# Attention over odd batches with its token chunks on the other half of the partitions

## The chip, the cores and the metric

One core of one Trainium2 chip runs the whole program. The metric is the device time of one execution in microseconds; of several runs the median counts. In the profile PE is TensorE's matmul side, PEld its weight loads, DVE VectorE, ACT ScalarE, POOL GpSimd and SP the engine that issues most DMAs.

## The reference

Three stages in a row. `_attn_ref` is a delta-rule attention over 4 batches, 8 heads, 768 tokens and head size 48; `_moe_ref` a gated feed-forward of width 1536 over the 3072 rows of 384; `_moe2_ref` sends every row to one of 8 experts.

```python
def _attn_ref(q, k, v, beta):
    k_n = k / (np.linalg.norm(k, axis=-1, keepdims=True) + 1e-06)
    state = np.zeros((B, H, D, D))
    for t in range(S):
        kt, vt, bt = (k_n[:, :, t], v[:, :, t], beta[:, :, t, None])
        y[:, :, t] = np.einsum('bhd,bhde->bhe', q[:, :, t], state)
        v_old = np.einsum('bhde,bhd->bhe', state, kt)
        state = state + bt[:, :, :, None] * np.einsum('bhd,bhe->bhde', kt, vt - v_old)

x = y.transpose(0, 2, 1, 3).reshape(B * S, H * D)
xn = x / rms(x) * rms_g                       # moe
x = (silu(xn @ w_gate) * (xn @ w_val)) @ w_out
e = argmax(x @ w_gate2)                       # moe2
out = softmax_e * sigmoid(x @ w_output_gate)_e * (relu(x @ w1[e]) @ w2[e])
```

## The kernel before

**Attention** takes 128 tokens of every head per step (6 steps, `m`), in two chunks of 64 (`ch`). The 32 heads are 16 pairs `q` in two groups `g` of 8; of a group, pairs 0 to 3 are of an even batch and 4 to 7 of an odd one. The two heads of a pair (`h`) lie on the two halves of the 128 partitions.

`early(m)` needs no state. It squares and sums the keys (`squares`), works out the keys' products (`gram` with `what == "k"`, 16 matmuls for each quarter `b` of the heads, called `gk` in the trace), and inverts the chunks' triangular matrices on VectorE (`solve`, L232 to L274: a transposition `nb`, a product, 31 rounds of `tmp` and `x`, four transpositions into `ng`). Four `corner` products (`off`) end it.

`late(m, g)` needs the state. It takes the products of keys and queries (`gq`), and then for each chunk the stages of `chain`: `z` (keys times state, 16 matmuls, then a VectorE subtraction into `v`), `u` (inverse times `v`, 16 matmuls, then two ScalarE copies into `right`), `y` (the output, 16 matmuls with all 128 rows of the array, two copies) and `s` (16 matmuls, two VectorE additions). A float32 matmul shows as two records, so a stage has 32.

Which part of TensorE's array a small matmul uses follows from its partitions: the operands' half gives the rows, the output's half the columns. In `gk` and `z` head 0 has the lower rows and the lower columns, head 1 the upper rows and the upper columns. In `u` it is the lower rows with the upper columns, and the reverse. So a stage goes between two of the four quarters. In `y` every matmul has all the rows, and the columns of half `to`, which is one and the same for the whole stage.

**The feed-forward** has 12 blocks of 256 tokens (`block`), 12 pieces `f` each: `up(f)` of 18 matmuls into `gv` (two PSUM buffers), then ScalarE (`th`, `val`), VectorE (`th`, L641), GpSimd (`th`, L642), ScalarE (`h`, L644), GpSimd (`h`, L645), and `down` of 6 matmuls into `po`. Per step of attention there are two blocks. `route` picks the expert and writes the rows to DRAM; at the end `Moe2` plans units of tokens per expert (`plan_full`, whose list of ids `lt_f` is gathered by GpSimd and transposed by TensorE as `pl_f`), fetches weights (`wraw`) and rows (`xg`), and multiplies.

What is emitted when is set by `Weave`, which counts TensorE's time as written in the yields (0.64 for a stage) and lets the side tasks step when their gap has passed. A scheduler then fixes the order of each engine, and every engine keeps its own order. The PSUM tag `at` has 4 banks, shared by all of attention, `xt`, `off` and `rk`; a `z`, `u` or `gk` takes one, a `y` two.

## Time and profile before

| | |
|---|---|
| runs | 1111.62, 1114.97, 1115.9 us (median 1114.97) |
| span of the profiled execution | 1112.2 us |
| PE busy | 1009.8 us, 91% |
| DVE busy | 692.9 us, 62% |
| ACT busy | 468.8 us, 42% |
| POOL busy | 457.0 us, 41% |

The page gives the span of the profiled execution, and not its time apart from that; the three runs lie from 0.6 us below to 3.7 us above this span, their median 2.8 us above it. The slices of the page show three parts: to about 130 us weights and the first inverse, with PE half busy; from there to about 835 us attention and feed-forward together, with PE at 98% and more from 300 us on; then the experts. Whoever reads it should not stay with the share of the whole span: in a stretch of the middle part VectorE is as full as TensorE, and the windows show which.

### The profile page before, as it was taken

The numbers are of one execution on the slowest core, as the hardware profiler recorded it, in microseconds if no ns is written. First come the engines' busy times: TensorE is split into PE (matmuls) and PEld (weight loads), VectorE is DVE, ScalarE is ACT, GpSimd is POOL, SyncE is SP. The second block draws the span as 40 slices with busy tenths as digits, with TensorE's granted clock in tenths as the row PEclk, the third lists the DMA queues.
The fourth block names the chain that finished last, engine by engine and source line by source line (L and its number), as shares of the span: only waits on it lengthen the run. The fifth ranks groups of instructions, "written<-read, shape, count | busy, mean of one in ns | idle before, by whom it ended". The sixth has DMA issues, their size and how long they took to land.

```text
span 1112.2 us, 27509 instructions
## 1 busy us (share of the span) xinstructions
PE 1009.8 (91%) x11189; PEld 953.3 (86%) x11189; DVE 692.9 (62%) x1954; ACT 468.8 (42%) x1193; POOL 457.0 (41%) x523
## 2 busy tenths in 40 slices
PE   5726898899999999999999999999999999999993
PEld 4725797788898989998999889999998889999993
DVE  5995889669833994389536973234418646557550
ACT  6626552353345334533354334333436434445440
POOL 9517443432544335433534243325653553212210
PEclk9999699899999999999999999999999899999997
DMA  9812750122302211220312130001404574355320
GB/s 290 218 58 75 207 114 1 34 70 44 73 16 45 58 45 45 58 59 16 72 45 45 31 72 16 2 2 64 165 1 146 174 236 153 130 192 190 115 99 15
DMA packets 53289, 97.04 MB, mean 87 GB/s; under 512 B 5792, under 2 KB 38198, under 8 KB 50338
## 3 DMA queue, kind: packets, MB, share of 16 engines
q1 hardware_dynamic: 43122, 48.76, 16.6%
q0 software_dynamic: 7680, 45.08, 11.7%
q8 instruction: 90, 1.47, 0.6%
q10 hardware_dynamic: 2352, 1.37, 0.4%
q14 instruction: 45, 0.37, 0.1%
HBM read 83.78 MB, written 12.09 MB: 86 GB/s over the span
## 4 chain that ended last, share of the span: by engine, by line
PE 49%; DVE 21%; issue 11%; POOL 7%; DMA 6%; ACT 4%; SPq 1%; POOLq 0%; ACTq 0%; DVEq 0%
PE gv L632 17%; PE po L655 8%; PE cpo L1010 8%; PE ph L989 8%; DVE tmp L253 5%; DVE x L257 5%; PE y L332 2%; POOL raw L520 1%; POOL th L642 1%; DVE th L641 1%; DMA sq<-in_kv_dram 1%; DVE left L223 1%; PE off L293 1%; DVE right L343 1%; POOL h L645 1%
## 5 line engine op out<-in xcount | busy, mean ns | idle before, releaser
L642 POOL TENSOR_TENSOR th<-th,val 128x256 f32<-128x256 f32 x144 | 111.1, 773 | 268.9 <-DVE th L641 227.9
L655 PE MATMUL po<-wout,h 128*128 128x400 f32 x864 | 192.4, 353 | 4.0 <-ACT h L644 2.8
L641 DVE SCALAR_TENSOR_TENSOR th<-th,gv 128x256 f32<-128x256 f32 x144 | 60.1, 417 | 176.3 <-ACT val L640 170.5
L644 ACT ACTIVATE h<-th 128x256 fp32r<-128x256 f32 x144 | 60.0, 417 | 241.3 <-POOL th L642 241.2
L632 PE MATMUL gv<-xh,wgv 128*128 128x256 f32 x864 | 150.0, 295 | 7.0 <-DVE th L641 6.8
L655 PEld LDWEIGHTS po<-wout,h 128*128 128x128 f32 x864 | 148.0, 189 | 8.9 <-ACT h L644 3.9
L632 PE MATMUL gv<-xh,wl 128*128 128x256 f32 x864 | 146.2, 287 | 3.3 <-DVE th L641 3.2
L645 POOL TENSOR_TENSOR h<-th,h 128x256 fp32r<-128x256 f32 x144 | 108.3, 753 | 73.6 <-ACT h L644 73.3
L632 PEld LDWEIGHTS gv<-xh,wgv 128*128 128x128 f32 x864 | 125.3, 197 | 10.4 <-DVE th L641 7.6
L632 PEld LDWEIGHTS gv<-xh,wl 128*128 128x128 f32 x864 | 122.9, 190 | 7.7 <-DVE th L641 5.6
L1010 PE MATMUL cpo<-w2h,ch 128*128 128x384 f32 (+1 forms) x464 | 124.2, 340 | 1.9 <-ACT w2h L950 1.9
L253 DVE TENSOR_TENSOR tmp<-nb,x 128x110 f32<-128x110 f32 (+35 forms) x366 | 106.4, 330 | 4.2
L989 PE MATMUL ph<-xT,w1h 128*128 128x256 f32 (+4 forms) x528 | 95.1, 315 | 0.1
L257 DVE TENSOR_TENSOR x<-x,tmp 128x110 f32<-128x110 f32 (+35 forms) x366 | 94.4, 295 | 0.3
L638 ACT ACTIVATE th<-gv 128x256 f32<-128x256 f32 x144 | 54.5, 378 | 79.5 <-PE gv L632 77.2
L1010 PEld LDWEIGHTS cpo<-w2h,ch 128*128 128x128 f32 (+1 forms) x464 | 81.8, 184 | 4.3 <-ACT w2h L950 2.5
L989 PEld LDWEIGHTS ph<-xT,w1h 128*128 128x128 f32 x528 | 82.9, 192 | 1.7 <-DVE ch L994 0.4
L632 PE MATMUL gv<-xl,wgv 128*128 128x256 f32 x432 | 79.6, 291 | 1.0 <-DVE xl L613 1.0
L1010 PE MATMUL cpo<-w2l,ch 128*128 128x384 f32 (+1 forms) x232 | 78.2, 338 | 0.0
L632 PE MATMUL gv<-xl,wl 128*128 128x256 f32 x432 | 77.0, 285 | 0.0
L632 PEld LDWEIGHTS gv<-xl,wgv 128*128 128x128 f32 x432 | 64.9, 197 | 1.9 <-DVE xl L613 1.4
L994 DVE SCALAR_TENSOR_TENSOR ch<-ph,ch 128x512 fp32r<-128x512 f32 (+4 forms) x64 | 39.0, 611 | 40.9 <-ACT ch L993 40.9
(241 smaller groups left out, 1841.8 us busy)
## 6 DMA issues: line engine op xcount, KB each, us to landing
kT<-in_kqT_dram SPq DMA_DIRECT2D x24, 192.0 KB, 3.8
raw<-in_wo_dram SPq DMA_DIRECT2D x12, 384.0 KB, 7.4
left<-in_kqT_dram SPq DMA_DIRECT2D x24, 192.0 KB, 4.2
v<-in_kv_dram SPq DMA_DIRECT2D x12, 384.0 KB, 3.4
k<-in_kv_dram SPq DMA_DIRECT2D x24, 192.0 KB, 4.9
raw<-in_wg_dram SPq DMA_DIRECT2D x12, 384.0 KB, 3.4
raw<-in_wv_dram SPq DMA_DIRECT2D x12, 384.0 KB, 4.3
rows<-y SPq DMA_DIRECT2D x10, 385.0 KB, 3.0
```

Source lines behind the costliest of these rows:

```text
L253: nc.vector.tensor_tensor(out=t, in0=nb[:, k + 1:, k:k + 1].to_broadcast([P, n, b - a]), in1=x[:, k:k + 1, a:b].to_broadcast([P, n, b - a] ...
L257: nc.vector.tensor_tensor(out=x[:, k + 1:, a:b], in0=x[:, k + 1:, a:b], in1=t, op=ALU.add)
L632: nc.tensor.matmul(out=ps[:, gv], lhsT=self.weight(wi, cc, gv, slice(f * P, f * P + P)), rhs=xx[:, cc], start=i == 0, stop=i == 8)
L638: nc.scalar.activation(out=th, in_=ps[:, 0], func=AF.Tanh, scale=0.5)
L641: nc.vector.scalar_tensor_tensor(out=th, in0=th, scalar=1.0, in1=ps[:, 0], op0=ALU.add, op1=ALU.mult)
L642: nc.gpsimd.tensor_tensor(out=th, in0=th, in1=val, op=ALU.mult)
L644: nc.scalar.activation(out=h2[:, 0], in_=th, func=AF.Copy)
L645: nc.gpsimd.tensor_tensor(out=h2[:, 1], in0=th, in1=h2[:, 0].bitcast(F32), op=ALU.subtract)
L655: nc.tensor.matmul(out=po[t], lhsT=h[:, ts], rhs=self.wo[wi][:, f], start=f == 0 and i == 0, stop=f == 11 and i == 2)
L989: nc.tensor.matmul(out=ph[:, fl], lhsT=w1[wi][:, cc, f * P:(f + 1) * P], rhs=xt[:, xi, cc], start=i == 0, stop=i == 8)
L994: nc.vector.scalar_tensor_tensor(out=hl, in0=ph, scalar=0.0, in1=hh.bitcast(F32), op0=ALU.max, op1=ALU.subtract)
L1010: nc.tensor.matmul(out=po[t][0:rows[t]], lhsT=hs[f // 2][:, hi, f % 2, t * P:t * P + rows[t]], rhs=w2[wi][:, f], start=f == 0 and i == 0, ...
```

## The change

For the heads of odd batches (pairs 4 to 7 of a group, `f` = 1 in the new code) the two heads' chunks lie on swapped halves of the partitions: in `v`, `k`, `ng`, the gram matrices, `beta`, the tokens' ids and the output `x`. The host arrays are reordered to fit. In `z`, `u` and the new `keygram` even and odd pairs then alternate over all four quarters of the array, each parity into a PSUM bank of its own; in `y` they alternate between the two halves of the columns. `keygram` does two quarters of the heads at once (32 matmuls, two banks). Nothing is added to or taken from the matmuls themselves. `gq`, `s` and `off` keep their pattern.

Around it: `z` is subtracted in two VectorE operations of half the size, `u` copied in four ScalarE operations of half the size, the keys `k` are loaded by three DMAs in place of two, the grams of step 1 by four in place of two, and a block's rows are written by three DMAs in place of one (step 0: four in place of two). The yield after the keys' products is 0.8 for both quarters (twice 0.64 before).

```diff
+    def keygram(self, m, g):
+        bank = [self.ps.tile([P, 8, 64], F32, tag="at", name=f"gk{m}{g}{f}") for f in range(2)]
+        for pl in range(4):
+            for ch in range(2):
+                for f in range(2):
+                    for h in range(2):
+                        kk = k[64 * h:64 * h + D, 4 * f + pl, 64 * ch:64 * ch + 64]
+                        o = 64 * (h ^ f)
+                        nc.tensor.matmul(out=bank[f][o:o + 64, 2 * pl + ch], lhsT=kk, rhs=kk, start=True, stop=True)
...
+        turns = [(i, f, 4 * f + i, h) for i in range(4) for f in range(2) for h in range(2)]
+        if stage in "zu":
+            bank = [self.ps.tile([P, 4, D], F32, tag="at", name=f"{stage}{m}{ch}{g}{f}") for f in range(2)]
         if stage == "z":
-            for q in range(GPR):
+            for i, f, q, h in turns:
+                nc.tensor.matmul(out=bank[f][own[h ^ f], i], lhsT=kT[sub[h], q, 64 * ch:64 * ch + 64],
+                                 rhs=R[sub[h], q, h], start=True, stop=True)
+            for f in range(2):
+                v = vn[:, 4 * f:4 * f + 4]
+                nc.vector.tensor_tensor(out=v, in0=v, in1=bank[f], op=ALU.subtract)
+        elif stage == "u":
+            for i, f, q, h in turns:
+                nc.tensor.matmul(out=bank[f][own[1 - h], i], lhsT=self.ng[own[h ^ f], 2 * (g * GPR + q) + ch],
+                                 rhs=vn[own[h ^ f], q], start=True, stop=True)
+            for f in range(2):
                 for h in range(2):
-            nc.vector.tensor_tensor(out=vn, in0=vn, in1=ps, op=ALU.subtract)
-            for h in range(2):
-                nc.scalar.activation(out=R[own[1 - h], :, h], in_=ps[own[1 - h]], func=AF.Copy)
+                    nc.scalar.activation(out=R[own[1 - h], 4 * f:4 * f + 4, h], in_=bank[f][own[1 - h]], func=AF.Copy)
...
-            o = own[to]
-            for q in range(GPR):
+            for i in range(4):
                 for h in range(2):
-                    nc.tensor.matmul(out=bank[q // 4][o, q % 4, h], lhsT=self.left[g][:, q, h, 64 * ch:64 * ch + 64],
-                                     rhs=R[:, q, h], start=True, stop=True)
+                    for f in range(2):
+                        q = 4 * f + i
+                        nc.tensor.matmul(out=bank[f][own[to ^ f], i, h],
+                                         lhsT=self.left[g][:, q, h, 64 * ch:64 * ch + 64],
+                                         rhs=R[:, q, h], start=True, stop=True)
...
-            nc.sync.dma_start(out=rows[m * P:(m + 1) * P, 2 * g:2 * g + 2], in_=y)
+            nc.sync.dma_start(out=rows[m * P:(m + 1) * P, 2 * g], in_=y[:, 0])
+            for h in range(2):
+                nc.sync.dma_start(out=rows[m * P + 64 * h:m * P + 64 * h + 64, 2 * g + 1],
+                                  in_=y[64 - 64 * h:128 - 64 * h, 1])
```

Three places in the engines' orders. On PE, the last step's inverse products of group 0 (`u`), before, among the feed-forward's `gv`:

```order
L632 MATMUL gv_7907<-xh_7559,wgv_82 128x256 x3
L319 MATMUL u_7917<-v_4_6576,ng 64x48 x16
L208 MATMUL gk_7936<-ek_5_7791 64x64 x16
L632 MATMUL gv_7907<-xh_7559,wgv_81 128x256 x3
L632 MATMUL gv_7907<-xl_7560,wgv_81 128x256 x3
```

and of the changed kernel, where `u_8046` and `u_8047` are the banks of the even and the odd batch:

```order
L659 MATMUL gv_8036<-xh_7626,wgv_82 128x256 x3
L340 MATMUL u_8046<-v_4_6675,ng 64x48 x2
L340 MATMUL u_8047<-v_4_6675,ng 64x48 x2
L340 MATMUL u_8046<-v_4_6675,ng 64x48 x2
L340 MATMUL u_8047<-v_4_6675,ng 64x48 x2
```

The 16 matmuls of `u` are now pairs that alternate between two banks, and the keys' products no longer follow them directly: both `keygram`s stand apart, the one ahead of this `u`, the other after the next `y`.

On DVE, the start of the last inverse, before: `nb` is its first transposition, `th` the feed-forward's product, one per piece `f`, and the last `th` here is that of piece 6 of block 7.

```order
L641 SCALAR_TENSOR_TENSOR th_8053<-th_8053,gv_8034 128x256
L343 TENSOR_TENSOR right_78<-right_78,s_8062 48x8x48 x2
L243 MEMSET x_8256 128x1024
L238 STREAM_TRANSPOSE nb_8170<-xr_7868 128x1024
L244 MEMSET x_8256 128x32
L240 TENSOR_TENSOR nb_8170<-nb_8170,naT_8144 128x1024
L314 TENSOR_TENSOR v_4_6576<-v_4_6576,z_8119 128x8x48
L253 TENSOR_TENSOR tmp_0_8277<-nb_8170,x_8256 128x31
L257 TENSOR_TENSOR x_8256<-x_8256,tmp_0_8277 128x31
L253 TENSOR_TENSOR tmp_1_8280<-nb_8170,x_8256 128x30 x2
L257 TENSOR_TENSOR x_8256<-x_8256,tmp_1_8280 128x30 x2
L641 SCALAR_TENSOR_TENSOR th_8155<-th_8155,gv_8109 128x256
```

and of the changed kernel, where `th_8185` is that of piece 5 and `th_8238` that of piece 6:

```order
L668 SCALAR_TENSOR_TENSOR th_8084<-th_8084,gv_8036 128x256
L263 MEMSET x_8389 128x1024
L264 MEMSET x_8389 128x32
L258 STREAM_TRANSPOSE nb_8292<-xr_7980 128x1024
L369 TENSOR_TENSOR right_78<-right_78,s_8194 48x8x48 x2
L668 SCALAR_TENSOR_TENSOR th_8185<-th_8185,gv_8122 128x256
L260 TENSOR_TENSOR nb_8292<-nb_8292,naT_8280 128x1024
L273 TENSOR_TENSOR tmp_0_8398<-nb_8292,x_8389 128x31
L668 SCALAR_TENSOR_TENSOR th_8238<-th_8238,gv_8219 128x256
```

The transposition has moved one piece earlier, while the rounds behind it stand about where they did.

On POOL, the fetches of the first plan after the last `y`, before (`lt_f` is the list of ids, `wraw` the experts' weights):

```order
L645 TENSOR_TENSOR h_10560<-th_10554,h_10560 128x256
L940 DMA wraw_10327<-in_w_dram,wi_f 128x3072
L940 DMA wraw_10328<-in_w_dram,wi_f 128x3072
L782 DMA lt_f<-list,li_f 6x128
L642 TENSOR_TENSOR th_10588<-th_10588,val_10590 128x256
```

and of the changed kernel:

```order
L672 TENSOR_TENSOR h_10713<-th_10707,h_10713 128x256
L813 DMA lt_f<-list,li_f 6x128
L971 DMA wraw_10480<-in_w_dram,wi_f 128x3072
L971 DMA wraw_10481<-in_w_dram,wi_f 128x3072
L669 TENSOR_TENSOR th_10741<-th_10741,val_10743 128x256
```

The list has moved ahead of the two weights. On PE, `pl_f`, which transposes it, stands 80 feed-forward matmuls after the last `y`, where 153 stood between them before.

## Rows read from the trace of the kernel before

**Rows 1.** The page: the span.

```profile
span 1112.2 us, 27509 instructions
```

**Rows 2.** Busy time by stretch: start:end, length, then each engine's us (instructions).

```profile
240.00:302.00 62.00, 60.21 (x766) 56.08 (x765) 59.77 (x189) 20.87 (x58) 22.82 (x27) 1.00 0.28 65
...
601.00:648.00 47.00, 45.32 (x524) 41.61 (x522) 45.90 (x169) 15.33 (x45) 15.38 (x20) 1.00 0.16 44
sum 206.00, PE 199.33 PEld 184.79 DVE 200.31 ACT 67.02 POOL 70.53; mean PE 49.83 PEld 46.20 DVE 50.08 ACT 16.75 POOL 17.63
...
648.00:770.00 122.00, 122.00 (x1583) 115.02 (x1583) 44.44 (x137) 47.36 (x127) 47.54 (x70) 1.00 0.09 21
```

**Rows 3.** Groups of PE instructions, 220 to 770 us: records, busy us, mean ns.

```profile
L332 PE MATMUL y<-right,left 128*64 128x48 f32 x640 | 44.0, 224 | 0.6 <-ACT right L322 0.2
L312 PE MATMUL z<-right,kT 48*64 48x48 f32 x626 | 24.4, 220 | 3.2 <-DVE right L343 2.9 <-DVE left L223 0.3
L319 PE MATMUL u<-v,ng 64*64 64x48 f32 x640 | 22.9, 220 | 1.1 <-DVE v L314 1.1
L208 PE MATMUL gk<-ek 48*64 48x64 f32 x512 | 19.1, 221 | 2.7 <-DMA ek<-in_kqT_dram 2.7
```

**Rows 4.** Timeline of PE, 584 to 594 us: start, length, rows*columns used, records.

```profile
584.95 0.96 PE L319 MATMUL u<-v,ng 64*64 64x48 f32 x26
585.70 0.27 PE L208 MATMUL gk<-ek 48*64 48x64 f32 x2
585.74 0.28 PE L319 MATMUL u<-v,ng 64*64 64x48 f32 x3
585.80 0.22 PE L208 MATMUL gk<-ek 48*64 48x64 f32 x1
585.81 0.22 PE L319 MATMUL u<-v,ng 64*64 64x48 f32 x1
585.81 0.22 PE L208 MATMUL gk<-ek 48*64 48x64 f32 x1
585.86 0.22 PE L319 MATMUL u<-v,ng 64*64 64x48 f32 x1
585.86 0.22 PE L208 MATMUL gk<-ek 48*64 48x64 f32 x1
585.87 0.22 PE L319 MATMUL u<-v,ng 64*64 64x48 f32 x1
585.87 0.98 PE L208 MATMUL gk<-ek 48*64 48x64 f32 x27
...
589.13 2.07 PE L332 MATMUL y<-right,left 128*64 128x48 f32 x32
591.12 1.15 PE L208 MATMUL gk<-ek 48*64 48x64 f32 x32
```

**Rows 5.** Timeline of PE, 409 to 428 us: a `u` and what follows.

```profile
411.17 1.14 PE L319 MATMUL u<-v,ng 64*64 64x48 f32 x32 [0.39 <-DVE v L314]
412.24 0.86 PE L632 MATMUL gv<-xh,wgv 128*128 128x256 f32 x5
```

**Rows 6.** The four stretches of Rows 2, instructions that use tile y alone.

```profile
sum 206.00, PE 20.18 PEld 18.05 DVE 3.34 ACT 10.32; mean PE 5.04 PEld 4.51 DVE 0.83 ACT 2.58
```

**Rows 7.** Timeline of PE and of POOL, 764 to 790 us: the last `y`, the plan.

```profile
764.65 1.83 PE L332 MATMUL y<-right,left 128*64 128x48 f32 x28
...
787.18 0.22 PE L791 MATMUL pl_f<-ident,lf_f 6*128 6x6 f32 x1
...
775.73 0.96 POOL L782 DMA_INDIRECT lt_f<-list,li_f  x1 [0.30 <-issue]
```

**Rows 8.** DMA issues: count and us to landing.

```profile
lt_f<-list,li_f POOLq DMA_INDIRECT x1, 8.1
lt_m<-list,li_m POOLq DMA_INDIRECT x1, 3.0
```

**Rows 9.** Timeline of PE, 95 to 119 us: a `y` of the first step.

```profile
96.85 4.91 PE L332 MATMUL y<-right,left 128*64 128x48 f32 x46
```

More of the change, by code (lines that the diff above doesn't have):

```diff
@@ L77, in load @@
             for h in range(2 if n > 0 else 0):
-                nc.sync.dma_start(
-                    out=self.left[g][64 - 64 * h:128 - 64 * h, 0:4 * n, h],
-                    in_=a["kq", m][64 * h:64 * h + 64, 16 * g:16 * g + 8 * n].rearrange("p (q c) t -> p q (c t)", c=2))
+                for f in range(n):
+                    o = 64 * (h ^ f)
+                    nc.sync.dma_start(
+                        out=self.left[g][64 - 64 * h:128 - 64 * h, 4 * f:4 * f + 4, h],
+                        in_=a["kq", m][o:o + 64, 16 * g + 8 * f:16 * g + 8 * f + 8].rearrange(
+                            "p (q c) t -> p q (c t)", c=2))
         else:
@@ L199, in gram @@
         g = b // 2
-        ps = self.ps.tile([P, 8, 64], F32, tag="at", name=f"g{what}{m}{b}")
-        k, left = T["early", g] if what == "k" else T["kT"][g], self.left[g]
+        ps = self.ps.tile([P, 8, 64], F32, tag="at", name=f"gq{m}{b}")
+        k, left = T["kT"][g], self.left[g]
         for pl in range(4):
@@ L364, in early @@
                 self.nc.sync.dma_start(out=T["raw"][1][r, ns], in_=self.a["kk", m][r, q % 2, ns])
-        for b in range(4):
-            if b >= n:
-                self.gram(m, b, "k")
-            if not ready:
-                self.roots(m, b)
-            yield (0.64 if b >= n else 0.0), eg
+        for g in range(2):
+            if 2 * g >= n:
+                self.keygram(m, g)
+            for b in (2 * g, 2 * g + 1):
+                if not ready:
+                    self.roots(m, b)
+            yield (0.8 if 2 * g >= n else 0.0), 2 * eg
         if not ready:
@@ L725, in route @@
         if m:
-            nc.sync.dma_start(out=rows[m * P:(m + 1) * P, 2 * g:2 * g + 2], in_=y)
+            nc.sync.dma_start(out=rows[m * P:(m + 1) * P, 2 * g], in_=y[:, 0])
+            for h in range(2):
+                nc.sync.dma_start(out=rows[m * P + 64 * h:m * P + 64 * h + 64, 2 * g + 1],
+                                  in_=y[64 - 64 * h:128 - 64 * h, 1])
         else:
             for h in range(2):
-                nc.sync.dma_start(out=rows[64 * g:64 * g + 64, 2 * h:2 * h + 2], in_=y[64 * h:64 * h + 64])
+                for t in range(2):
+                    nc.sync.dma_start(out=rows[64 * g:64 * g + 64, 2 * (h ^ t) + t], in_=y[64 * h:64 * h + 64, t])
         run = small("run", [P, 2, 8])
@@ L1070, in constants @@
     iota("cnt0", [P, 8], [[NT, 8]], 0, 0)
[L1071 removed]
+    c["tok"] = pool.tile([P, NM, 2, 2], I32, name="tok")
     c["tok0"] = pool.tile([P, 2, 2], I32, name="tok0")
     for h in range(2):
[L1075 removed]
+        p = slice(64 * h, 64 * h + 64)
+        for t in range(2):
+            nc.gpsimd.iota(c["tok"][p, :, :, t], pattern=[[P, NM], [2 * S, 2]], base=64 * (h ^ t) + S * t,
+                           channel_multiplier=1, allow_small_or_imprecise_dtypes=True)
+        nc.gpsimd.iota(c["tok0"][p], pattern=[[64, 2], [-S if h else 3 * S, 2]], base=2 * S * h, channel_multiplier=1,
                        allow_small_or_imprecise_dtypes=True)
```

62 lines of the change are left out of this document (29 added, 33 removed).

## The prediction, as put on record

> **What bounds the kernel now.** I read the windows first, since the share of the whole span mixes stages. From 220 to 770 us, where attention and feed-forward run together, TensorE is full: in the last 122 us before the attention ends it is busy for all of them, VectorE for 44 [rows 2]. There a microsecond off TensorE is a microsecond off the kernel. But in four stretches, 206 us in all, one per inverse of steps 2 to 5, VectorE is busy for 200.3 us and TensorE for 199.3 [rows 2]. The reader is to see that both are at 97% there: what is taken from TensorE is then waited for at VectorE, since `gv` has two buffers and each piece `f` needs VectorE's `th`. So the first question is how much shorter the small matmuls get, the second where they stand.
>
> **What a stage costs, and why.** A `u` of 32 records starts at 411.17, and the next matmul at 412.24: 1.07 us [rows 5]. Within a stage 26 records take from 584.95 to 585.70, 28.8 ns each [rows 4], so 32 of them are 0.92 us, and 0.15 us is what a stage loses at its end. `y` takes 1.99 us for 32 records (589.13 to 591.12), and with 0.13 to 0.15 us at its end 58 ns each: twice the time of `u` for as many columns streamed [rows 4]. `u` goes between two quarters of the array, `y` stays in one half of the columns. That is the pattern of a cost per place in the array of 58 ns per record, of which two places hide each other's.
>
> **Would four places hide four?** The trace holds the experiment by accident. Where `gk` follows `u` directly, the last `u` and the first `gk` run mixed. `u` uses the two quarters that `gk` doesn't. From 585.70 to 585.87 start 2+3+1+1+1+1+1+1 = 11 records, 15.5 ns each [rows 4], against 28.8 while `u` is alone just before and (585.87 on, 27 records of `gk`) again just after. Four quarters work at once, and two that share their rows and differ in columns don't hold each other up. The rate is 15.5 / 28.8 = 0.54 of that of two, near a half.
>
> The Trainium skill's page "TensorE: Matmul & The Clock Gate" (Part 3, "The mechanism") has a rule against this change: weight loads overlap running matmuls only where the row groups differ. By it `y`, whose matmuls have all the rows, gains nothing, and `z`, `u` and `gk`, which change rows already, little; the kernel would stay at about 1115. The mixed records above speak against that rule for the quarters; for `y`, with all 128 rows, no row here shows it.
>
> **The change part by part.**
>
> *`z` and `u`.* 32 records at 15.5 ns are 0.50 us, with 0.15 at the end 0.65, against 1.07: 0.42 saved; at an exact half 0.46. I take 0.43. From 220 to 770 us there are 626 / 32 and 640 / 32, so 20 of each [rows 3]: 40 x 0.43 = 17.2 us.
>
> *`y`.* The trace has no `y` that alternates columns. The bounds are 0 (the all-rows matmul doesn't overlap) and 32 x 29.2 + 150 ns = 1.08, so 0.91 saved of 1.99. It is nearest to the mixed rows, where tiles that share rows and differ in columns run side by side, so I take 0.54 of the rate with some loss, 0.88. 20 of them [rows 3]: 17.6 us.
>
> *`gk`.* 512 / 32 = 16 stages [rows 3] become 8 of double size. Two are 2 x 1.07; the double one is 64 x 15.5 + 150 ns = 1.14: 1.0 saved; where a `gk` mixed with its neighbour before, some 0.15 of that was had already. I take 0.9: 7.2 us.
>
> Together 42.0 us of TensorE's time between 220 and 770.
>
> *What VectorE takes back.* In the four stretches lie 20.18 of the 44.0 busy us of `y` [rows 3, 6], 46%; by the order `z` and `u` lie there in much the same share, while all `gk` lie outside (the inverse comes after them). 0.45 x (17.2 + 17.6) = 15.7 us of the saving falls where VectorE has 200.3 of 206 us to do. At most 5.7 us of idle can go there. I take 2, because its rounds have waits of their own, and because the first transposition of each inverse now stands one piece earlier, where VectorE has room. So 42.0 - 15.7 + 2 = 28.3 us. The ends: 42.0 - 15.7 = 26.3 if nothing is recovered, 42.0 if the inverse's operations spread over the pieces so that nothing binds.
>
> *The first step.* Its `u`, `y` and `z` stand before 150 us. One `y` run takes 4.9 us there for 46 records [rows 9], so 2 to 4 us could go; but VectorE and the weights decide when the first block begins. Bounds 0 and 4, I take 1.5.
>
> *The plan.* `pl_f` ran at 787.18, 20.7 us after the last `y` ended (764.65 + 1.83) [rows 7], and TensorE did 153 feed-forward matmuls in between, 0.135 us each. Now 80 stand between: 10.8 us. TensorE's queue stops there until the list is in, and the feed-forward behind it waits too. But the list's fetch, issued at 775.73 and 8.1 us on its way behind two weight fetches, is now ahead of them; the one like it later took 3.0 us [rows 7, 8]. Issued some 2.7 us earlier and landing 5 us sooner, and without the split of the weights that VectorE did ahead of its copy, it comes about 11 us after the last `y`. Cost 0 to 10 us, I take 1.
>
> *The small pieces.* Two half subtractions for one and four half copies for two add an operation's fixed part each; `u` to `y` is still over 20 matmuls of 0.135 us apart, and the same holds from `z` to `u`, so they are hidden outside the stretches. Inside them one more VectorE operation for each of some 9 `z` is below 1 us. The DMAs stand in SP's queue: three for `k` instead of two, three for a block's rows instead of one; ahead of them SP mostly waits for data, and only the last block's rows are on the path, for two more issues. I take 0.5 for all.
>
> Sum: 28.3 + 1.5 - 1 - 0.5 = 28.3 us. From the span of 1112.2 [rows 1] this gives 1083.9, and with the 2.8 us by which the median of the runs lies above it, **1087 us**.
>
> **The rivals.**
>
> *`y` gains nothing* (12 in 100). All rows are taken by each matmul, so the column halves might follow each other. Outside the stretches that takes away 0.55 x 17.6 = 9.7 us: 1096. For it: no row shows such a pair. Against: the quarters that share rows overlap.
>
> *VectorE doesn't bind* (14 in 100). Its rounds are filler whose place the order sets; if they spread over more pieces, all 42 us go, and up to 4 at the start: 1115 - 46 = 1069. For it: in the last 122 us VectorE is at 36% [rows 2], and the inverse begins earlier. Against: in the new order the rounds stand between the same pieces as before.
>
> *The columns don't overlap at all* (10 in 100). What the mixed records show might be an effect of two tiles of different stages. Then only the small costs are left: 1113 to 1118. Against: the rate changes with the first mixed record and returns with the last [rows 4].
>
> *The banks run out* (5 in 100), on the other side. `z`, `u` and `gk` now hold two of the four `at` banks, `y` two as before, so a stage can only start when the one before the last is evacuated. In the stretches VectorE is behind, and holds the banks of `gq` and `z`. 48 stages are affected; from a mean wait of 28.3 / 48 = 0.6 us on, the gain is gone, and at 0.8 us each (38 us) the time is 1125. For it: VectorE is 97% busy where it must free them. Against: `y` takes two banks right after `u` today, with 0.6 us of idle over all `y` [rows 3], and the stages stay over 20 matmuls apart.
>
> The page "TensorEngine Tiling (Array Packing)" of the Trainium skill ("PSUM Bottleneck") says the same in general: tiling speeds up TensorE and not the evacuation, which may become the bound. Here the trace shows VectorE full in 206 of 550 us, by other work than evacuation.
>
> **How the numbers follow.** My forecast has 59 in 100, with its own range of 1076 to 1095 (half of the recoverable cases on either side, the plan's wait above). The range for 8 in 10 reaches from 1067, just below the case in which VectorE doesn't bind, to 1104, beyond that of `y` without gain; what is left out is mostly the 15 in 100 of no overlap and of the banks. A measurement here tells 0.5%, 5.6 us, from no change. Faster by more than that: 59 + 12 + 14 = 85 in 100; within it: 10; slower: 5.
>
> **What would show it.** In the profile of the changed kernel `z` and `u` should take 0.6 to 0.7 us from their first record to the next stage's (1.07 before), `y` 1.05 to 1.2 (1.99), a double `gk` 1.05 to 1.2. If `y` stays at 2.0 it is the first rival; if all stay, the third. The four stretches should still last about as long as before, with VectorE at 97% and more, and TensorE at 90% or less in them, idle before `gv` and `z` with VectorE as the releaser. The 122 us that end at 770 should shrink by about 4 x 0.43 x 2 + 5 x 0.88 = 8 us. `pl_f` should follow the last `y` by 11 to 12 us, with less than 2 us of idle before it. I am wrong if TensorE waits for banks (idle before `z`, `u` or `gk` released by an evacuation), if the stretches shrink by more than 6 us in all, or if the inverse now ends so late that `off` waits.

## The result, and the profile after

The changed kernel takes 1123.53 us (1120.97 to 1125.13, 6 runs) against 1115.16 us (1111.31 to 1118.29, 6 runs) for the kernel before: ratio 1.0076, 95% interval 1.0054 to 1.0097. It is slower by 8.4 us where 28 us of gain were forecast, and the forecast range of 1067 to 1104 doesn't hold it.

The page of the changed kernel, span and engines, for [rows 1]:

```profile
span 1121.0 us, 27686 instructions
...
PE 990.6 (88%) x11189; PEld 926.9 (83%) x11189; DVE 702.3 (63%) x1976; ACT 473.7 (42%) x1241; POOL 458.4 (41%) x526
```

The window from 220 to 770 us, first the kernel before, then the changed one (columns as in [rows 2], the third from the end is the mean granted clock):

```profile
220.00:770.00 550.00, 539.00 (x7241) 502.69 (x7237) 335.78 (x1047) 219.33 (x591) 222.56 (x274) 1.00 0.17 42
```
```profile
220.00:770.00 550.00, 513.53 (x7079) 472.49 (x7070) 339.31 (x1040) 218.99 (x617) 222.03 (x262) 0.96 0.18 41
```

TensorE is busy for 25.5 us less in the same 550 us, at a granted clock of 0.96 in place of 1.00. The two windows don't hold quite the same work, so I also took the account between the same two feed-forward pieces, from VectorE's `th` of piece 6 of block 1 to that of piece 0 of block 10. That part took 529.6 us and takes 536.1. TensorE's busy time in it went from 518.6 to 500.5, idle from 11.0 to 35.7; and of the 500.5, up to 19.9 us are lost to clocks below 1.00 (an estimate: one minus the granted clock, summed over TensorE's busy time; 1.7 before). So 18.1 + 18.2 = 36 us of work at full clock were taken away, less than the 42 forecast, and 24.7 us of idle and 18.2 of lower clock took their place. Some 3 of the 36 us are no saving: a `u` and two of the keys' stages that lay in this part now run ahead of it.

The small matmuls themselves. Groups of PE's instructions between 220 and 777 us, changed kernel, for [rows 3]:

```profile
L355 PE MATMUL y<-right,left 128*64 128x48 f32 x640 | 32.5, 235 | 11.7 <-ACT right L344 11.3
L333 PE MATMUL z<-right,kT 48*64 48x48 f32 x608 | 17.0, 223 | 5.0 <-DVE left L243 3.4 <-DVE right L369 1.6
L340 PE MATMUL u<-v,ng 64*64 64x48 f32 x640 | 15.5, 224 | 2.4 <-DVE v L337 2.4
L215 PE MATMUL gk<-ek 48*64 48x64 f32 x451 | 10.5, 247 | 2.0 <-DMA ek<-in_kqT_dram 2.0
```

And single stages on PE's timeline, changed kernel, for [rows 4, 5]:

```profile
354.91 1.15 PE L355 MATMUL y<-right,left 128*64 128x48 f32 x32
355.99 1.16 PE L215 MATMUL gk<-ek 48*64 48x64 f32 x64
357.08 0.39 PE L659 MATMUL gv<-xl,wl 128*128 128x256 f32 x1
...
583.81 0.68 PE L333 MATMUL z<-right,kT 48*64 48x48 f32 x32
584.42 1.35 PE L682 MATMUL po<-wout,h 128*128 128x400 f32 x6
...
588.06 0.68 PE L340 MATMUL u<-v,ng 64*64 64x48 f32 x32
588.67 0.62 PE L659 MATMUL gv<-xh,wgv 128*128 128x256 f32 x3
```

`z` and `u` go from 1.07 to 0.61 us from their first record to the next matmul, `y` from 1.99 to 1.08, and a double `gk` takes 1.09 where two took 2.14. That is what was forecast, where a stage finds its operands and the full clock. The last column of the groups holds the other half: 11.7 us of idle before `y`, where the kernel before had 0.6. PE's waits from 220 to 772 us, changed kernel (what waits, for which engine's product; us in all, times, longest):

```profile
PE y L355 <- ACT right L344: 11.3, 7, 7.5
PE gv L659 <- DVE th L668: 5.3, 4, 2.1
PE po L682 <- ACT h L671: 3.7, 5, 1.4
PE xt L632 <- DVE x L621: 3.4, 4, 1.5
PE z L333 <- DVE left L243: 3.4, 4, 1.4
PE po L682 <- POOL h L672: 2.7, 3, 2.3
PE u L340 <- DVE v L337: 2.4, 5, 0.7
PE gk L215 <- DMA ek<-in_kqT_dram: 2.0, 2, 1.1
PE z L333 <- DVE right L369: 1.6, 2, 1.4
```

These nine sum to 35.8 us. The same list of the kernel before sums to 10.2 us, its longest entry being

```profile
PE z L312 <- DVE right L343: 2.9, 3, 1.1
```

No single wait took the gain; they are spread over ScalarE, VectorE and GpSimd.

Where in the program? I compare the starts of the same feed-forward `th` in both traces. From piece 3 of block 0 to the middle of block 1 the changed kernel is ahead (by 2.7 us at the start of block 1). The four stretches with an inverse, measured between the same pieces, took 206.8 us before and take 219.1: 12.3 us more, in order of time 0.6, 2.4, 4.9 and 4.4. Between them it gains only 5.7 us in all, where 26 were forecast. At the last piece of the feed-forward it is 7.4 us behind, at the end of the span 8.8. The two windows that answer to the last rows of [rows 2], a stretch and the time after it:

```profile
604.00:653.00 49.00, 43.26 (x508) 39.49 (x508) 46.96 (x167) 15.22 (x46) 16.26 (x20) 0.93 0.16 42
653.00:777.00 124.00, 120.44 (x1601) 112.14 (x1601) 47.95 (x149) 49.32 (x138) 49.41 (x71) 0.97 0.09 21
```

VectorE is busy for 47 of 49 us of the stretch, as before, while TensorE is at 43 and its clock at 0.93. Pieces 6 of block 7 to 4 of block 8, which hold this stretch, took 49.8 us and take 54.2.

### The profile page after: what moved, and what is told of

The parts are those of the page before. It is cut to its first block, busy times and chain, and to the rows that moved or that the text cites. A ratio compares the mean times of both kernels' runs of the same rounds, so it can differ in the third digit from the quotient of the medians.

```text
span 1121.0 us, 27686 instructions
## 1 busy us (share of the span) xinstructions
PE 990.6 (88%) x11189; PEld 926.9 (83%) x11189; DVE 702.3 (63%) x1976; ACT 473.7 (42%) x1241; POOL 458.4 (41%) x526
## 4 chain that ended last, share of the span: by engine, by line
PE 43%; DVE 25%; issue 13%; POOL 7%; ACT 6%; DMA 5%; POOLq 0%; SPq 0%; ACTq 0%; DVEq 0%
PE gv L659 13%; PE cpo L1041 8%; PE ph L1020 7%; PE po L682 7%; DVE tmp L273 6%; DVE x L277 6%; POOL th L669 2%; DVE th L668 2%; PE y L355 2%; DVE right L369 1%; POOL raw L547 1%; POOL h L672 1%; ACT xr L221 1%; PE off L310 1%; PE gq L236 1%
## 5 line engine op out<-in xcount | busy, mean ns | idle before, releaser
L669 POOL TENSOR_TENSOR th<-th,val 128x256 f32<-128x256 f32 x144 | 114.4, 795 | 264.8 <-DVE th L668 198.5
L682 PE MATMUL po<-wout,h 128*128 128x400 f32 x864 | 198.8, 361 | 10.6 <-ACT h L671 7.4
L682 PEld LDWEIGHTS po<-wout,h 128*128 128x128 f32 x864 | 151.3, 194 | 18.6 <-ACT h L671 9.4
L659 PE MATMUL gv<-xh,wl 128*128 128x256 f32 x864 | 148.8, 292 | 9.5 <-DVE th L668 9.4
L659 PEld LDWEIGHTS gv<-xh,wl 128*128 128x128 f32 x864 | 125.8, 195 | 14.6 <-DVE th L668 12.7
L277 DVE TENSOR_TENSOR x<-x,tmp 128x110 f32<-128x110 f32 (+35 forms) x366 | 101.9, 315 | 0.2
L665 ACT ACTIVATE th<-gv 128x256 f32<-128x256 f32 x144 | 54.2, 376 | 74.8 <-PE gv L659 71.9
```

The costliest lines, as they stand in the source:

```text
L277: nc.vector.tensor_tensor(out=x[:, k + 1:, a:b], in0=x[:, k + 1:, a:b], in1=t, op=ALU.add)
L659: nc.tensor.matmul(out=ps[:, gv], lhsT=self.weight(wi, cc, gv, slice(f * P, f * P + P)), rhs=xx[:, cc], start=i == 0, stop=i == 8)
L665: nc.scalar.activation(out=th, in_=ps[:, 0], func=AF.Tanh, scale=0.5)
L669: nc.gpsimd.tensor_tensor(out=th, in0=th, in1=val, op=ALU.mult)
L682: nc.tensor.matmul(out=po[t], lhsT=h[:, ts], rhs=self.wo[wi][:, f], start=f == 0 and i == 0, stop=f == 11 and i == 2)
```

## The experiments

All ratios are against the kernel before, run beside it on the same chip; us are worked out from them with 1115. Chips differ by up to 14 us (medians of the kernel before from 1115 to 1129), so spans from different chips aren't set side by side. The starts of feed-forward pieces are: what follows the last piece takes 278 to 283 us in the traces of the faster chips and 288 to 292 in those of the slower, so most of the difference lies there.

### The turns, and what came with them

**paired** keeps the new layout, the two banks and the double `keygram`, but runs the even batch's matmuls first and then the odd one's:

```diff
-        turns = [(i, f, 4 * f + i, h) for i in range(4) for f in range(2) for h in range(2)]
+        turns = [(i, f, 4 * f + i, h) for f in range(2) for i in range(4) for h in range(2)]
```

(and `f` outermost in `keygram` and `y`).

> The changed kernel with the turns taken back in all four kinds of stages: the layout, the half-size copies and subtractions, the double gk and the DMAs stay, but the matmuls of f = 0 come first and those of f = 1 after them, so only two parts of the array (in y one half of the columns) are used in turn. Theory A (the turns do save TensorE's time, and the idle time that the rest of the change brings eats it): z and u go back to about 1.07 us, y to 2.0, TensorE is busy for some 40 us more, and the kernel is slower than the changed one: 1130 to 1145. Theory B (outside TensorE's queue other engines set the pace everywhere, so TensorE's time is worth nothing): 1119 to 1127, as the changed one. Theory C (the turns themselves do the harm, since a TensorE that waits loses its clock): faster than the changed one, 1112 to 1118.

Measured: 1.0232 [1.0199, 1.0266]. The stages don't go all the way back: undisturbed, `z` and `u` take 0.88 us and a double `gk` 1.84, and a `y` 1.80 (PE, `paired`):

```profile
631.36 1.87 PE L355 MATMUL y<-right,left 128*64 128x48 f32 x32
633.16 1.36 PE L682 MATMUL po<-wout,h 128*128 128x400 f32 x6
```

So between 220 and 770 us the turns alone shorten TensorE's stages by some 31 us (an estimate: 40 x 0.27 + 20 x 0.72 + 8 x 0.75), and the new places alone by the rest. In the kernel's time the turns are a gain, of 1.0232 − 1.0076 = 1.56%, 17.4 us. But everything else in the change costs 2.3%, 26 us, where the prediction had 1.5 (the plan and the small pieces). Some 13 us of what the turns give is had in the first step: at piece 4 of block 0, `paired` is 11.4 us behind the kernel before and the changed kernel 1.5 ahead. There it is the order that differs, and not only the length of the stages: in `paired` the second `u`, both `y` and `s` stand in a row on TensorE, from 137 to 149 us, where the kernel before and the changed one have feed-forward matmuls among them. From there to the last piece the turns are worth 5.6 us more.

Two experiments take one of the other parts alone, without turns, into the kernel before. **before_2bank** gives `z` and `u` two banks and the halved operations behind them:

```diff
-                    nc.tensor.matmul(out=ps[own[h], q], lhsT=kT[sub[h], q, 64 * ch:64 * ch + 64],
+                    nc.tensor.matmul(out=bank[q // 4][own[h], q % 4], lhsT=kT[sub[h], q, 64 * ch:64 * ch + 64],
```

> The kernel before, in its own layout and with no turns, but z and u write the first four heads' pairs to one bank and the last four to another, with two half subtractions and four half copies, as the changed kernel has to. If the second bank of z is what it waits for (z of the later heads then needs the bank of the second gq, which VectorE frees with the mask that stands behind the inverse's rounds): idle time before z of some 10 us, and 1.006 to 1.012 of the time before. If the half operations and the banks are hidden: 0.998 to 1.003.

Measured: 1.0122 [1.0091, 1.0153], 13.6 us. Of that 8.6 us are there by piece 4 of block 0, where the second `u`, both `y` and `s` now run ahead of the feed-forward, as in `paired`. The waits that I expected before `z` are there, at about half of the size, released by the operation that empties `gq`'s bank (PE's waits, 220 to 772 us, `before_2bank`):

```profile
PE z L314 <- DVE left L223: 5.8, 4, 2.0
```

But they cost nothing where they stand: from piece 6 of block 1 to piece 0 of block 10 this kernel takes 528.7 us, the kernel before 529.6. Another 4.5 us come between that piece and the last. So most of the price arises in step 1, with an order that came with the second bank, and none of it from these waits.

**before_gk2** lets the plan take two of the keys' stages in one step, as the changed kernel does:

```diff
-        for b in range(4):
-            if b >= n:
-                self.gram(m, b, "k")
-            if not ready:
-                self.roots(m, b)
-            yield (0.64 if b >= n else 0.0), eg
+        for g in range(2):
+            for b in (2 * g, 2 * g + 1):
+                if b >= n:
+                    self.gram(m, b, "k")
...
+            yield (0.8 if 2 * g >= n else 0.0), 2 * eg
```

> The kernel before with one edit: two stages of gk are issued in one step of the plan, as the double gk is, each with its bank, copies and places as before, and no turns. If the row of copies and norm steps that comes of it is what the double gk costs: idle time of 5 to 12 us before y with ScalarE as the releaser, 1.005 to 1.012. If it is the double gk's two banks and turns that matter, or nothing: 0.998 to 1.003.

Measured: 1.0098 [1.0063, 1.0134], 10.9 us. Together 24.5 us, about the 26 of `paired`. My expectation of where was wrong, though: `y` doesn't wait here. PE's largest wait in this kernel is for something else, and 6.9 of the 10.9 us lie in the four stretches, which take 213.7 us in place of 206.8:

```profile
PE po L657 <- ACT h L646: 6.5, 6, 2.4
```

### The lump of copies on ScalarE

The longest single wait of the changed kernel is the 7.5 us of a `y` at 230.61. The timelines of POOL, ACT and PE around it, changed kernel, in order of time:

```profile
223.23 3.23 POOL L127 TENSOR_TENSOR nrm<-ss,half 128x8 f32<-128x8 f32 x2 [1.03 <-DVE ss L106]
226.43 0.72 POOL L669 TENSOR_TENSOR th<-th,val 128x256 f32<-128x256 f32 x1
```
```profile
227.18 0.42 ACT L671 ACTIVATE h<-th 128x256 fp32r<-128x256 f32 x1 [4.34 <-POOL th L669]
227.50 0.64 ACT L218 ACTIVATE xr<-gk 128x256 f32<-128x256 f32 x2
...
230.23 1.37 ACT L344 ACTIVATE right<-u 64x192 f32<-64x192 f32 x4
```
```profile
230.61 0.45 PE L355 MATMUL y<-right,left 128*64 128x48 f32 x2 [7.50 <-ACT right L344]
```

The reader is to see a queue, not a slow engine. Two steps of the norms stand on GpSimd ahead of the feed-forward's `th`; ScalarE's `h` waits 4.34 us for it; behind `h` stand the eight copies of a double `gk`, 2.7 us; only then comes the copy of `u` for which `y` waits. Two variants take the lump apart.

**ksplit** makes four single `gk` of the two double ones, each with its own step and yield as before; `z`, `u` and `y` keep their turns:

```diff
-        for g in range(2):
-            if 2 * g >= n:
-                self.keygram(m, g)
-            for b in (2 * g, 2 * g + 1):
+        for b in range(4):
+            if b >= n:
+                self.keygram(m, b // 2, b % 2)
...
-            yield (0.8 if 2 * g >= n else 0.0), 2 * eg
+            yield (0.64 if b >= n else 0.0), eg
```

> The changed kernel with the double gk taken apart again: four stages of gk a step, each with one bank, its four copies and its own step in the plan, as before; z, u and y keep their turns. Theory A1 (the double gk puts eight copies in a row into ScalarE's queue, ahead of the copies of u for which y waits, and two norm steps in a row into GpSimd's): the idle time before y with ScalarE as the releaser falls from 11.3 us to under 3, and the kernel comes to 1104 to 1112, faster than both, although gk costs TensorE 7 us more. Theory A2 (the loss is in the four stretches where VectorE is full, and in the clock there): the idle time before y falls too, but the time stays at 1116 to 1124.

**kevict** keeps the 32 matmuls together and takes only the copies and the norms by halves:

```diff
+        for b in range(4):
+            if b >= n:
+                if b % 2 == 0:
+                    bank = self.keygram(m, b // 2)
+                self.keyraw(m, b // 2, b % 2, bank[b % 2])
```

> The changed kernel with the double gk kept, so that its matmuls go to four places in turn, but its copies and norm steps issued by halves, the second half a step of the plan later, as before. If ScalarE's eight copies and GpSimd's two norm steps in a row are what the double gk costs: like ksplit or better by up to 6 us, 0.993 to 1.001 of the time before, idle time before y under 3 us. If it is the place of the double gk in TensorE's order or the two banks that it holds: 1.004 to 1.010, as the changed kernel.

Measured: `ksplit` 0.9998 [0.9979, 1.0017], `kevict` 0.998 [0.9956, 1.0003]. In `ksplit` the time fell between its two ranges, and `kevict` kept the wait that I expected to go. So a plan step with two stages in it costs 0.8 to 1.0% whether the matmuls are shorter or not. But the lump at 230 us is not where it costs. In `ksplit` all waits of `y` are 1.7 us; in `kevict` that one wait stays (7.7 us), and the time is as good. By the pieces' starts the three kernels part late: at piece 6 of block 7 the changed kernel is 2.0 us behind the kernel before, `ksplit` 2.8 behind and `kevict` 0.4 ahead; at piece 0 of block 9 the changed kernel is 10.5 behind, `ksplit` 1.0 behind and `kevict` 0.6 ahead. The last two stretches take 54.5 and 54.2 us in the changed kernel, 50.2 and 50.0 in `ksplit`, 50.9 and 51.4 in `kevict`. The longest wait was thus not the dearest. How the plan's step lengthens a stretch was not shown.

### VectorE's inverse

The prediction let VectorE's work be a fixed amount per stretch. Three kernels leave out every second round of the inverse's loop in steps 2 to 5 (`x` is then not the inverse; the experts' part has as many matmuls as before):

```diff
+            if k % 2 and m > 1:
+                yield 0.34 + 2 * n * (k + 1) * 1.04e-3
+                continue
```

**light_before**, **light_after** and **light_ksplit** are this edit in the kernel before, the changed one and `ksplit`.

> The kernel before, with every second round of the inverse's loop left out on VectorE in steps 2 to 5 (the inverse is then not the right one; nothing else is left out), so that VectorE has some 13 us less to do in each of the four stretches. If the stretches are bound by VectorE, TensorE close behind: 5 to 8 us faster than before, 1107 to 1110, then TensorE binds them. If they weren't bound by VectorE: 1115.

> The same edit in the changed kernel. Theory A2 (the stretches where VectorE is full eat the gain): the changed kernel now gains what its shorter stages give, so 20 us or more below the kernel before with the same edit: 1080 to 1092. Theory A1 (the double gk's copies and the first step's chain eat it): some 15 us of the stretches are gained at most, 1100 to 1108, with the idle time before y still over 8 us.

> Both at once: four single gk a step as in ksplit, and every second round of the inverse's loop left out on VectorE in steps 2 to 5 (the inverse is then not the right one). If the idle time has two separate causes, ScalarE's row of gk copies and VectorE's full stretches, both are now gone: idle time of TensorE from 223 us to the end of the attention under 15 us, hardly any stretch at the half clock, and 0.975 to 0.983 of the time before. If taking one away only moves the waiting to the other: 0.988 to 0.992, no better than light_after at 0.991.

Measured: 0.9958 [0.9931, 0.9985], 0.9913 [0.9885, 0.9941], 0.9959 [0.9938, 0.9981]. Taking away the same work is worth 0.4% in the kernel before, 1.6% in the changed one (1.0076 to 0.9913, 18 us) and 0.4% in `ksplit` (0.9959 is outside both of its ranges). So the inverse holds the changed kernel up more than the kernel before. But half an inverse less doesn't bring 28 us, and in `ksplit` it hardly helps: there something else holds TensorE.

### The banks

In `ksplit` that is a wait of `z`. PE and DVE, timeline of `ksplit`:

```profile
505.97 0.43 PE L331 MATMUL z<-right,kT 48*64 48x48 f32 x6
...
510.35 1.09 PE L331 MATMUL z<-right,kT 48*64 48x48 f32 x26 [3.95 <-DVE left L241]
```
```profile
508.81 1.39 DVE L241 TENSOR_TENSOR left<-gq,maskU 64x512 f32<-64x512 f32 x2
```

The stage starts, runs six records, and stops for 3.95 us in the middle. The releaser is `left`, which `z` doesn't read: what it does is to empty `gq`'s bank. So `z` waits for that bank; that it is the second of its two, and that the kernel before needs only an earlier `gq`'s, fits, but no view here shows it. PE's waits in `ksplit`:

```profile
PE z L331 <- DVE left L241: 11.8, 4, 5.0
```

**ksplit_mask** takes that release from VectorE: `gq` is copied by ScalarE and masked by GpSimd.

```diff
-            if m:
+            if m < 0:
```

> ksplit with the mask of gq moved from VectorE to a copy on ScalarE and a select on GpSimd, as the first step has it, in all steps; that takes 2.75 us off VectorE in each of the stretches where it is full, and the copies that z waits for no longer stand behind the inverse's rounds. If VectorE's fullness is the cause of the waits before z (11.8 us in ksplit): those go, and the time falls by 6 to 12 us, to 0.989 to 0.995. If GpSimd, which has gate products to do that the next matmuls wait for, becomes the one that is waited for: 1.000 or above.

Measured: 1.0068 [1.0047, 1.0089], slower than `ksplit`. The wait stayed and changed its releaser, timeline of PE in `ksplit_mask`:

```profile
517.63 0.32 PE L331 MATMUL z<-right,kT 48*64 48x48 f32 x4
521.68 1.09 PE L331 MATMUL z<-right,kT 48*64 48x48 f32 x28 [3.74 <-ACT left L246]
```

That shows what `z` waits for (whoever empties `gq`), and that ScalarE's queue is no better a place for it.

**y_only** is `ksplit` with the turns of `z` and `u` taken back and their banks kept:

```diff
-            for i, f, q, h in turns:
+            for i, f, q, h in [(i, f, 4 * f + i, h) for f in range(2) for i in range(4) for h in range(2)]:
```

> ksplit with the turns of z and u taken back too, so that only y goes to both halves of the columns in turn. z and u go back to 1.07 us, 17 us of TensorE's time. If TensorE's time still counts in ksplit outside the stretches where VectorE is full (about half of z and u): 5 to 10 us slower than ksplit, 1.004 to 1.009 of the time before. If other engines set the pace: within 2 us of ksplit, 0.998 to 1.002.

Measured: 1.0104 [1.0076, 1.0132]. The turns of `z` and `u` are worth 1.06%, 12 us, and some 9 of them lie in the first step (`y_only` is 11 us behind the kernel before at piece 4 of block 0, `ksplit` 1.8). There `y_only` has the order of `paired` and `before_2bank`, the second `u`, both `y` and `s` in a row; all three have two banks and no turns in `z` and `u`. What that order costs by itself was not isolated.

### The order on VectorE

What is left is the order: in the stretches the rounds of the inverse, mere filler, stand ahead of `th` and of the mask in VectorE's queue, and a TensorE that comes sooner finds them there. The **paced** kernels forbid an operation of the inverse of steps 2 to 5 to be placed ahead of the last `th` that was emitted before it:

```diff
-        for t in self.solve(m):
+        acc, rounds = 0, self.solve(m)
+        while True:
+            with self.tc.issue_after(PACE["th"]) if m > 1 else nullcontext():
+                t = next(rounds, None)
...
-            nc.vector.scalar_tensor_tensor(out=th, in0=th, scalar=1.0, in1=ps[:, 0], op0=ALU.add, op1=ALU.mult)
+            PACE["th"] = nc.vector.scalar_tensor_tensor(
+                out=th, in0=th, scalar=1.0, in1=ps[:, 0], op0=ALU.add, op1=ALU.mult).ins
```

> The changed kernel with nothing left out, but the inverse's operations of steps 2 to 5 may not stand ahead of the feed-forward piece's th that was emitted last before them; so VectorE does the inverse over 11 pieces a step and not 7 or 8, and nearly up to the corner's matmuls. If the stretches where VectorE is full are where the gain goes: they disappear, th no longer lags, hardly any half clock after 300 us, and the time comes below light_after's 0.991, 0.978 to 0.989. If the two banks or ScalarE's queue are the larger cause: 0.990 to 1.005; if the corner now waits for the inverse, above that, with idle time before off.

> The same edit in the kernel before. TensorE has little idle time to give back there (10 us from 220 us on): 0.991 to 0.998, and as the control: what after_paced has below it is what the change is worth where VectorE doesn't bind.

> The inverse held back, and all turns taken back as in paired. Where VectorE doesn't bind the turns should be worth what the stages lose, 40 us and more of TensorE's time less what falls on other waits: paired_paced 30 to 42 us slower than after_paced, 1.016 to 1.026. If they are worth only the 17 us that lie between paired and the changed kernel: 1.002 to 1.006.

> Both mends: the inverse held back to the feed-forward's th as in after_paced, and gk in four single stages a step as in ksplit. If the idle time of 16 us before y that after_paced still has comes from the eight gk copies in a row: under 6 us of it are left, less time at the half clock, and 0.978 to 0.985 of the time before, although gk costs TensorE 7 us more. If that idle time is cover for other waits: 0.986 to 0.993, as after_paced.

> The inverse held back, and the double gk with its copies and norm steps issued by halves. If the halves come apart in ScalarE's queue: like ksplit_paced or up to 7 us better, 0.974 to 0.984. If they still stand in a row there (in kevict they did in the first step): like after_paced, 0.985 to 0.992.

| kernel | as it was | paced |
|---|---|---|
| before | 1 | 1.0013 [0.9988, 1.0039] |
| paired (no turns) | 1.0232 | 0.9994 [0.9972, 1.0016] |
| changed kernel | 1.0076 | 0.9886 [0.982, 0.9952] |
| ksplit | 0.9998 | 0.9878 [0.9844, 0.9912] |
| kevict | 0.998 | 0.9839 [0.9802, 0.9875] |

The same edit does nothing for the kernel before, where I expected 0.2 to 0.9%, and is worth 1.9% in the changed one. `paired_paced` came out below both of its ranges; `ksplit_paced` has the time of its second case, though its waits of `y` are 2.6 us as in the first. Pieces 6 of block 7 to 4 of block 8 take 49.8 us before, 54.2 in the changed kernel, 46.5 paced; pieces 6 of block 5 to 4 of block 6 take 49.6, 54.5 and 46.5. All four take 191.4 us in `after_paced`, 27.7 less than in the changed kernel; that is the whole gain of the edit, 25 us at the last piece. So the stretches weren't of fixed length: an inverse can be spread, and then they shrink. A window of `kevict_paced` inside the last inverse's loop, for the one of 604 to 653 us above:

```profile
601.00:648.00 47.00, 45.80 (x579) 42.65 (x577) 40.71 (x148) 17.01 (x51) 19.34 (x25) 1.00 0.23 48
```

VectorE is busy for 40.7 of 47 us rather than 47.0 of 49, TensorE for 45.8, and the clock is at 1.00. One inverse's loop now lasts 53 to 57 us in place of 43 to 45. The waits for the bank went too: in `after_paced`, idle before `z` is 0.3 us in all. Hence the paced kernels don't tell VectorE's `th` from VectorE's mask; what they show is that it was the place of the inverse in its queue (the edit names VectorE's operations alone, though the other engines' orders move a little with it). Not all of the loss went: between piece 6 of block 1 and piece 0 of block 10, `after_paced` still has 17.7 us of idle, most of it before `y`, and up to 14.7 of lower clock, where the changed kernel has 35.7 and 19.9. `paired_paced` says the same of the banks: without turns, pacing alone wins back nearly all of the 2.3%.

`kevict_paced` is the best version here, 0.9839 of the kernel before, about 18 us of the 28 forecast. PE's longest wait in it, 7.1 us of a `y`, is still that of step 1, which the edit leaves alone.

**Open.** By medians the turns are worth 1.1% under pacing (0.9994 and 0.9886); in the two traces the last feed-forward piece differs by 25 us, 14 of them in the first step. The profiled run of `paired_paced` was its longest (1134.4 us, median 1127.9), and the interval of `after_paced` is wide, so how much of the 42 us is paid out can't be said better than between 12 and 25. What the lower clock costs by itself was not isolated. A kernel with `z` in one bank for both parities was not tried.

## Why the prediction failed, step by step

**What bounds the kernel.** Half right. That TensorE is full between the stretches and VectorE in them was read rightly from [rows 2]. The step that failed is the sentence after it, "There a microsecond off TensorE is a microsecond off the kernel." My reading is that TensorE was full since the other engines' queues had been ordered against its old pace, each a little ahead of it. With the stages shorter, the products of the other engines came a little too late in many places: PE's waits rose from 10.2 to 35.8 us, and up to 18 us more went to the clock. That `paced`, which constrains nothing but VectorE's order, gives 1.9% back in the changed kernel and nothing in the kernel before shows it for that queue; for the others it is argued.

**The stages, 42.0 us.** Right where nothing disturbs them. Undisturbed, `z` and `u` take 0.61 us (forecast 0.65), `y` 1.08 (taken as 1.11, 0.88 saved, with 1.08 as its bound), a double `gk` 1.09 (1.14 worked out). In place part of it was lost again, and 36 us of work at full clock went by the account above, 3 of them only moved: the `y` of 220 to 772 us take 31.1 us in all after 42.2, and not 24.6. The rival "`y` gains nothing" and the rival "no columns overlap" fell. So did the rule of the Trainium skill that stood against the change, "TensorE: Matmul & The Clock Gate", Part 3, "The mechanism": by it only matmuls in different row groups hide each other's weight loads. `y` has all 128 rows in every matmul and now takes 1.08 us per 32 records in place of 1.99, by nothing but its columns.

**VectorE takes back 15.7.** The direction was right and the size wrong. The sum was 42.0 less 13.7 taken back; by the account above it was 36 less 43, the 24.7 us of idle and 18.2 of lower clock. I held the stretches at their length. They grew by 12.3 us, since the waits there are not only VectorE's total: the inverse's loop got longer too, 45.1 and 44.7 us for the last two against 40.9 and 41.0. In the sum, the stretches were to give about 2 us and took 12, the rest was to give 26 and gave 6.

**`gk`, 7.2 saved.** Costed on TensorE alone. Its term in the diff's other half, a plan step with two stages' copies and norms in it, was not in the sum at all: 10.9 us by `before_gk2`, 8.7 by `ksplit`. The diff showed it (`yield 0.8`, `2 * eg`), and the cost showed in the stretches, which the prediction held fixed.

**The small pieces, 0.5.** The second bank was costed as hidden and as a rival of 5 in 100. `before_2bank` prices it, with the halved operations, at 13.6 us. My argument against, "the stages stay over 20 matmuls apart", looked at the chain of the stages; in the waits that did come the bank is held by `gq`, of another chain. The halved copies had a price as well, for which see the last section. The rival's time is near (1125 us against 1123.5), but that is luck: its 48 waits of 0.8 us are not what the trace shows. Idle before `z`, `u` and `gk` is 9.4 us in the changed kernel, and 8.6 of the 13.6 us arise in the first step, with an order that the changed kernel doesn't have.

**First step 1.5, plan −1.** The first step is 1.5 us ahead at piece 4 of block 0, as forecast, but by luck: without turns the second bank comes with another order there and some 9 us, and the turns undo both. For the plan, [rows 7, 8], changed kernel:

```profile
770.08 1.44 PE L355 MATMUL y<-right,left 128*64 128x48 f32 x30
...
782.34 0.22 PE L822 MATMUL pl_f<-ident,lf_f 6*128 6x6 f32 x1
```

`pl_f` follows the end of the last `y` by 10.8 us (11 to 12 forecast), with no idle before it. From piece 0 of block 10 to the end of the span the changed kernel falls back by 3.1 us, of which the plan's part can't be told.

**What would show it.** "I am wrong if TensorE waits for banks" is what happened in part, and the clock's fall in the stretches was in no case of mine.

## What to carry to other kernels

When TensorE is full, ask how far ahead of it each other queue runs before counting its saving: a wait before 0.6 us of work can be worth more than the work. Price what a change brings along (a second bank, two stages in one plan step) by a variant that has that part alone in the old kernel; here each cost a whole per cent. Then look where the time goes, by the starts of the same piece in both traces: the longest wait was not where it went. And where one engine carries filler for later and products that are needed now, fix that order before making the engine that waits for it faster.

## What was not expected of the hardware

**The clock falls after a stretch of short waits.** Consecutive windows inside a stretch with an inverse, changed kernel:

```profile
506.00:508.00 2.00, 1.41 (x7) 0.74 (x5) 1.97 (x5) 1.39 (x5) 1.31 (x2) 1.00 0.00 0
508.00:510.00 2.00, 1.26 (x12) 0.87 (x12) 1.92 (x7) 0.33 (x1) 0.00 (x0) 1.00 0.00 0
510.00:512.00 2.00, 0.67 (x24) 0.57 (x24) 2.00 (x8) 0.00 (x0) 0.69 (x1) 1.00 0.00 0
512.00:514.00 2.00, 1.31 (x4) 1.31 (x5) 1.97 (x8) 0.42 (x1) 1.04 (x2) 0.50 0.01 4
514.00:516.00 2.00, 2.00 (x10) 1.99 (x9) 1.97 (x12) 0.00 (x0) 0.00 (x0) 0.50 0.00 0
```

TensorE idles for 2.7 of six us, behind a VectorE that is full, and then has work again, but at 0.50, 1.2 GHz in place of 2.4, for the 2 us windows from 512 to 518. The wait is paid a second time there. It is the same with the `y` that waited 7.5 us: its last 30 records take 2.07 us, at a granted clock of 0.50, where 30 records at full clock take 1.15:

```profile
231.30 2.07 PE L355 MATMUL y<-right,left 128*64 128x48 f32 x30 [0.25 <-ACT right L344]
...
287.75 1.15 PE L355 MATMUL y<-right,left 128*64 128x48 f32 x30
```

**A stage that starts before all its operands are there is slow, and the profile calls it busy.** Three `y` take 1.99 us at full clock, as long as in the kernel before. One of them, PE and ACT:

```profile
593.04 2.06 PE L355 MATMUL y<-right,left 128*64 128x48 f32 x32 [1.23 <-ACT right L344]
595.03 0.62 PE L659 MATMUL gv<-xh,wgv 128*128 128x256 f32 x3
```
```profile
592.66 1.37 ACT L344 ACTIVATE right<-u 64x192 f32<-64x192 f32 x4
```

It starts behind the first of ScalarE's four copies and runs into the others, which end at 594.03. Its first eight records are up to 256 ns apart, and then most go at 58 ns for two, the full rate. So 0.9 us are a wait that shows as busy time, and here the halved copies let a stage start early to no gain.

**The inverse's long operations all have GpSimd beside them.** One case in the inverse's loop, DVE and POOL, changed kernel:

```profile
488.74 0.25 DVE L273 TENSOR_TENSOR tmp<-nb,x 128x96 f32<-128x96 f32 x1
488.91 2.24 DVE L277 TENSOR_TENSOR x<-x,tmp 128x96 f32<-128x96 f32 x2
```
```profile
488.78 0.80 POOL L672 TENSOR_TENSOR h<-th,h 128x256 fp32r<-128x256 f32 x1 [0.53 <-DMA v<-in_kv_dram]
489.55 1.48 POOL L147 TENSOR_TENSOR v<-v,nrm 128x768 f32<-128x768 f32 x1
```

Two updates of 0.25 us each take 2.24 us, as long as GpSimd's two products beside them. In the six loops 87 operations of the changed kernel are over 0.5 us (77 before), every one of them beside an operation of GpSimd, 0.85 us in the mean against 0.25 for the rest; of those with nothing of GpSimd beside them none is over 0.30. The Trainium skill gives a reason in "SBUF — State Buffer" ("SBUF: two separate sides"): the two engines share a pair of ports, and one that holds it locks the other out for a whole instruction. This trace agrees, and it is why VectorE's busy time is no fixed amount: it depends on what stands beside it.
